# Attention work of three successive tiles emitted at one place of a fused attention and gated-MLP kernel

## The chip, the cores and the metric

The kernel runs on one core of a Trainium2 chip. The metric is the device time in microseconds (us) of one execution; before the change it is 1166.69 us, the median of 3 runs (1166.23 to 1167.01). Five engines run side by side, each with its own queue of instructions in order: TensorE (PE: matmuls; PEld is its weight load), VectorE (DVE), ScalarE (ACT), GpSimd (POOL) and SyncE (SP, which issues the DMA transfers). They wait for each other through semaphores.

## What is computed

Chunked attention with memory keys, a gated MLP with a sigmoid gate and a second MLP that multiplies by its own sigmoid, in float32:

```python
# attention: 4 batches, 8 heads, 768 tokens, head dimension 64
for c in range(24):                            # chunks of 32 queries
    k_full = concat(mem_k, k[c*32-16 : c*32+40])   # 8 + 56 keys at most
    v_full = concat(mem_v, v[c*32-16 : c*32+40])
    s = q_c @ k_full.T / 8
    a = exp(s - max(s)); a = a / (sum(a) + 1e-9)
    out_c = a @ v_full
# first MLP: 3072 tokens, 512 -> 1536 -> 512
y = (sigmoid(x @ w_gate) * (x @ w_val)) @ w_out
# second MLP: 3072 tokens, 512 -> 2048 -> 512
h = y @ w_in;  result = (h * sigmoid(h)) @ w_out2
```

## The kernel before

**Tiles and blocks.** The 3072 tokens are 24 attention tiles of 128 tokens (six to a sequence, so the tiles 0, 6, 12 and 18 begin one) and six token blocks of 512, block 0 to block 5 (`bi`), of four tiles each. The attention of block 0 runs at the start. After that the first MLP runs block by block, and the attention of the four tiles of block `bi + 1` is interleaved with the MLP of block `bi`. The second MLP follows at the end, with nothing of the attention in it. Weights arrive as 64-bit numbers and are joined, and float32 values are split into two parts (a cast on ScalarE, then a subtraction, `split`), so that three matmuls of part times part stand for one product.

**A round.** For a block, a loop of 12 rounds runs over the slices `f` of the 1536 hidden columns. A round emits, in this order: the gate projection (`pg`, 12 wide matmuls of 128x512, L263) and its sigmoid on ScalarE (L273); step 0; the value projection (`pv`, 12 wide matmuls, L263); step 1; the gate product on VectorE (`sg<-pv,sg`, L277) and its split; the output matmuls of the round before (`y`, 12 wide matmuls, L90, L92, L94); step 2. So a block has 36 steps. `pg` and `pv` share a PSUM ring of two buffers (`ps_m`): a gate projection can begin when the sigmoid of the round before has read its buffer, a value projection when the gate product of the round before has.

**Head of a block.** In round 0 the output matmuls complete the previous block. Directly behind them the four finished tiles are copied from PSUM to SBUF, two by ScalarE (L530) and two by VectorE (L532), and stored (L533). These copies take their buffers from the same ring of three (`sg`) as the sigmoids; VectorE's second copy and the next sigmoid wait until a store has freed a buffer.

**Steps.** A step first runs its attention events (`run_events`), then, in block 0, the preparation of the first MLP's weights, and from block 1 on, in steps 1 and 2 of a round, one piece of the preparation of the second MLP's weights (`prepare2`). These pieces follow each other in a cycle of seven: a join, a join, four sums, and four half splits. A join is a rescale on ScalarE (L107) and three VectorE instructions (L115, L118, L122); the sums are four VectorE instructions (L478); a half split is a cast on ScalarE, a subtraction on VectorE and a store on SP (L486, or L492 with two DMAs). The half splits use one buffer (`co`), so a cast waits until the store before it has landed.

**Attention events of a tile.** Four kinds, at steps that `events` fixes:
- scores: 16 small matmuls into a PSUM tile `sc` (L189; tiles at the edge of a sequence get a mask, L197, L199), on VectorE the maximum (L202) and a subtraction into `e` (L203), on ScalarE the exponential (L204, for which ScalarE loads another function table than for the sigmoid); then two loads on SP, queries and keys of the next tile;
- norm: row sum, add, reciprocal and multiplication on VectorE (L210 to L213);
- turn: four transposes of `e` on TensorE into a PSUM tile `pt` (L219), copied by ScalarE to `at` (L220);
- pv: 16 small matmuls of `at` with the values into a PSUM tile `px` (L229), transposed into the block's input by VectorE (L236); then two loads on SP, values of the next tile. In the text below this is called the product, to keep it apart from the value projection.

The tiles `sc`, `pt` and `px` come from one PSUM ring of two buffers (`ps_a`); `e`, `at`, and the loaded queries, keys and values have one buffer each.

**What sets the order.** The schedule is manual: each engine's queue holds its instructions in the order in which the program emits them. Before the change tile `jj` of a block has its scores at step 3 + 8 `jj`, norm at 5 + 8 `jj`, turn at 7 + 8 `jj` and product at 9 + 8 `jj`. No two events share a step.

Of the kernel before, what the change touches and what calls it, by code (L numbers as in the profile page):

```python
# [23 lines left out]
NF1, NF2 = FF1 // P, FF2 // P  # L24
# [23 lines left out]
def moe_kernel(ctx: ExitStack, tc: tile.TileContext, qh, kh, vh, wg, wv, wo, w2i, w2o, out):  # L48
# [132 lines left out]
    def att_scores(t, ps_sc, e):  # L181
        sc = ps_sc(f"sc{t}")
        scv = sc.rearrange("p (c2 a k) -> p c2 a k", c2=2, a=4)
        qb, kt = q_t.pop(t), k_t.pop(t)
        for c2 in range(2):
            for a in range(4):
                for cp in range(2):
                    c = 2 * c2 + cp
                    nc.tensor.matmul(  # L189
                        scv[cp * 64 : cp * 64 + 64, c2, a],  # L190
                        qb[:, 4 * a + c].rearrange("p u q -> p (u q)"),
                        kt[:, a, c],
                        start=True,
                        stop=True,
                    )
        if t % TPB == 0:
            nc.vector.memset(scv[0:64, 0, :, NMEM : NMEM + LEFT], NEG)  # L197
        if t % TPB == TPB - 1:
            nc.vector.memset(scv[64:128, 1, :, WIN - RIGHT : WIN], NEG)  # L199
        s3 = sc.rearrange("p (g k) -> p g k", k=WIN)  # L200
        m = att.tile([P, 8, 1], F32, tag="m", name=f"m{t}", bufs=2)
        nc.vector.tensor_reduce(m, s3, axis=AX.X, op=ALU.max)  # L202
        nc.vector.tensor_tensor(out=e, in0=s3, in1=m.to_broadcast([P, 8, WIN]), op=ALU.subtract)  # L203
        nc.scalar.activation(out=e, in_=e, func=AF.Exp, scale=SCALE)  # L204
        e_t[t] = e

    def att_norm(t, eng=nc.vector):
        e = e_t[t]
        r = att.tile([P, 8, 1], F32, tag="r", name=f"r{t}", bufs=2)
        nc.vector.tensor_reduce(r, e, axis=AX.X, op=ALU.add)  # L210
        nc.vector.tensor_scalar_add(r, r, 1e-9)
        nc.vector.reciprocal(r, r)
        eng.tensor_tensor(out=e, in0=e, in1=r.to_broadcast([P, 8, WIN]), op=ALU.mult)  # L213

    def att_turn(t, ps_pt, at):
        e = e_t.pop(t).rearrange("p g k -> p (g k)")
        pt = ps_pt(f"pt{t}")
        for i in range(4):
            nc.tensor.transpose(pt[:, i * P : (i + 1) * P], e[:, i * P : (i + 1) * P], ident)  # L219
        nc.scalar.copy(at.rearrange("p a b q -> p (a b q)"), pt)  # L220
        at_t[t] = at

    def att_pv(t, ps_px, xt, off):
        at, vb = at_t.pop(t), v_t.pop(t)
        px = ps_px(f"px{t}")
        for c in range(4):
            for j in range(4):
                q0 = 64 * (c % 2) + 32 * (j % 2)
                nc.tensor.matmul(  # L229
                    px[32 * j : 32 * j + 32, c * P : (c + 1) * P],  # L230
                    at[:, c // 2, j // 2, q0 : q0 + 32],
                    vb[c * len(vb) // 4][:, :, c % (4 // len(vb)), j],
                    start=True,
                    stop=True,
                )
        nc.vector.transpose(  # L236
            out=xt[:, :, off : off + P].rearrange("p k (c q) -> p c k q", c=4),
            in_=px.rearrange("p (c k q) -> p c k q", c=4, k=4),
        )
# [3 lines left out]
    def x32_tile(name):  # L243
        return hold[0].tile([P, KT, 512], F32, tag="x32", name=name)
# [38 lines left out]
    with tc.manual_schedule():  # L283
# [17 lines left out]
        def at_tile(t):  # L301
            return att.tile([P, 2, 2, P], F32, tag="at", name=f"at{t}", bufs=1)

        def e_tile(t):
            return att.tile([P, 8, WIN], F32, tag="e", name=f"e{t}", bufs=1)
# [7 lines left out]
        for t in range(1, n0):  # L313
            i = 5 + 2 * (t - 1)
# [62 lines left out]
        def prefetch(t):  # L377
            if t < NTILE:
                att_load_qk(t, qA, k_tile(t))

        def prefetch_v(t):
            if t < NTILE:
                att_load_v(t, vA)

        idle(22)
        for i in range(n0 + 2):
# [3 lines left out]
            if 0 <= i - 2 < n0:  # L390
                at = hold[0].tile([P, 512], F32, tag="sg", name=f"at{i - 2}", bufs=3)
# [26 lines left out]
        events = {}  # L418
        for bi in range(NB1 - 1):
            n = BLOCKS1[bi + 1] // P  # L420
            for jj in range(n):
                t = starts1[bi + 1] // P + jj
                at = 3 * NF1 * bi + 3 + 24 * jj // max(n - 1, 1)
                for d, what in ((0, "scores"), (2, "norm"), (4, "turn"), (6, "pv")):
                    events.setdefault(at + d, []).append((what, t, bi + 1, jj))

        def run_events(i):
            for what, t, bn, jj in events.get(i, []):
                if what == "scores":
                    att_scores(t, ps_a, e_tile(t))  # L430
                    prefetch(t + 1)
                elif what == "norm":
                    att_norm(t)
                elif what == "turn":
                    att_turn(t, ps_a, at_tile(t))
                else:
                    if bn not in x32:
                        x32[bn] = x32_tile(f"x32_{bn}")
                    att_pv(t, ps_a, x32[bn], jj * P)
                    prefetch_v(t + 1)  # L440
# [179 lines left out]
        turn = [0]  # L620
# [181 lines left out]
        for bi, n in enumerate(BLOCKS1):  # L802
# [6 lines left out]
            for f in range(NF1):  # L809
                it = 3 * (bi * NF1 + f)  # L810

                def steps(i):
                    run_events(it + i)
                    if bi == 0:
                        feed1.step()
                    elif (it + i) % 3 != 0:
                        next(prep, None)
                    if last and (i == 2 and 1 < f < NF1):

                        if f >= 3:  # L820
                            next(xgen, None)
# [117 lines left out]
```

## Time and profile before

| | us |
|---|---|
| median of 3 runs | 1166.69 |
| lowest, highest | 1166.23, 1167.01 |
| the profiled execution | 1165.85 |
| span of its instructions | 1164.1 |
| TensorE busy in the span | 1138.2 |
| VectorE, ScalarE, GpSimd busy | 695.6, 487.4, 124.5 |
| mean granted clock of TensorE, as a share of full speed | 0.996 |

The profile is of one execution on the chip. Times of instructions are in us from the start of the span. Matmuls are pipelined, and their ends are modelled: the cost of one in a row of many is the distance from start to start, not its duration. A bracket behind a row of the timeline is the time its engine sat idle before it, and what ended that.

### The profile page before, as it was taken

Reading aid. Unit: us, or ns where it says so; the run is one execution under the profiler, and the core shown is the slowest. Engines: PE = TensorE matmul, PEld = TensorE weight load, DVE = VectorE, ACT = ScalarE, POOL = GpSimd, SP = SyncE. Lnnn points to the kernel's source line nnn. Section 1 sums busy time; section 2 is a strip of 40 time slices with the busy share of each in tenths; the row PEclk is TensorE's granted clock in tenths of the full one; section 3 lists DMA queues with packets and bytes.
Section 4 is the critical chain, followed back from the end, with each engine's and each line's share of the span. In section 5 each row is a group of like instructions: output and inputs, shape, how many; then the busy total and the mean of one; then the engine's idle time right before and its main releaser. Section 6 shows DMA issues by size and latency. Waiting matters only on the chain.

```text
span 1164.1 us, 16020 instructions
## 1 busy us (share of the span) xinstructions
PE 1138.2 (98%) x6319; PEld 927.7 (80%) x6319; DVE 695.6 (60%) x965; ACT 487.4 (42%) x708; POOL 124.5 (11%) x94
## 2 busy tenths in 40 slices
PE   8889999999999999999999999999999999999998
PEld 7667777888888888888887888888888888888887
DVE  7999965455555554554564534347944369634665
ACT  3555544334434433443343224445434454344442
POOL 2545530000000000000000001111001110011000
PEclk9999999999999999999999999999999999999999
DMA  9777767667656666766565356566655575655552
GB/s 314 244 238 246 242 218 238 208 206 227 224 194 212 219 227 194 242 213 203 199 205 211 120 188 199 190 239 237 228 199 192 205 282 215 227 193 203 208 204 86
DMA packets 79210, 248.51 MB, mean 213 GB/s; under 512 B 7584, under 2 KB 23968, under 8 KB 69920
## 3 DMA queue, kind: packets, MB, share of 16 engines
q1 hardware_dynamic: 79136, 247.49, 62.4%
q8 instruction: 50, 0.82, 0.3%
q14 instruction: 24, 0.20, 0.0%
HBM read 199.23 MB, written 48.23 MB: 213 GB/s over the span
## 4 chain that ended last, share of the span: by engine, by line
PE 83%; DVE 12%; DMA 3%; issue 1%; ACT 0%; SPq 0%; DVEq 0%; ACTq 0%
PE o L771 20%; PE c L658 20%; PE pv L263 13%; PE pg L263 13%; PE y L90 5%; PE y L92 5%; PE y L94 5%; PE sc L189 1%; PE px L229 1%; DVE t_wg L122 1%; DVE t_wo L122 1%; DVE t_wv L122 1%; DVE stg_wv L118 1%; DVE stg_wo L118 1%; DVE stg_wg L118 1%; DMA v<-in_vh_dram 1%
## 5 line engine op out<-in xcount | busy, mean ns | idle before, releaser
L658 PE MATMUL c<-xp,wr 128*128 128x512 f32 x1008 | 229.1, 389 | 0.0
L771 PE MATMUL o<-gf,wr 128*128 128x512 f32 x1008 | 229.0, 389 | 0.0
L263 PE MATMUL pv<-x,w 128*128 128x512 f32 x864 | 216.1, 400 | 13.0 <-DVE sg L277 11.4
L658 PEld LDWEIGHTS c<-xp,wr 128*128 128x128 f32 x1008 | 189.2, 188 | 39.3
L771 PEld LDWEIGHTS o<-gf,wr 128*128 128x128 f32 x1008 | 189.2, 188 | 39.3
L263 PE MATMUL pg<-x,w 128*128 128x512 f32 x864 | 210.6, 392 | 1.6 <-POOL x L85 0.9
L263 PEld LDWEIGHTS pv<-x,w 128*128 128x128 f32 x864 | 162.9, 191 | 51.9 <-issue 14.3
L263 PEld LDWEIGHTS pg<-x,w 128*128 128x128 f32 x864 | 160.4, 188 | 38.2 <-ACT x L82 1.5
L85 DVE TENSOR_TENSOR gf<-g,gf 128x1024 fp32r<-128x1024 f32 x84 | 103.8, 1239 | 49.9 <-ACT gf L82 49.6
L82 ACT CAST gf<-g 128x1024 fp32r<-128x1024 f32 x84 | 88.1, 1053 | 86.9 <-PE o L771 73.3
L678 POOL TENSOR_TENSOR s<-s,s 128x512 f32<-128x512 f32 x24 | 35.9, 1497 | 820.7 <-ACT s L677 820.7
L82 ACT CAST g<-sg 128x512 fp32r<-128x512 f32 x72 | 44.7, 621 | 156.8 <-DVE sg L277 156.8
L273 ACT ACTIVATE sg<-pg 128x512 f32<-128x512 f32 x72 | 42.9, 596 | 74.8 <-PE pg L263 61.7
L630 DVE TENSOR_TENSOR s<-c,s 128x512 f32<-128x512 f32 x48 | 33.2, 691 | 65.1 <-PE c L658 63.1
L90 PE MATMUL y<-g,wor 128*128 128x512 f32 x240 | 66.3, 397 | 0.6 <-DVE y L532 0.6
L85 DVE TENSOR_TENSOR g<-sg,g 128x512 fp32r<-128x512 f32 x60 | 41.5, 692 | 41.7 <-ACT g L82 41.7
L92 PE MATMUL y<-g,wor 128*128 128x512 f32 x240 | 64.3, 390 | 0.0
L94 PE MATMUL y<-g,wor 128*128 128x512 f32 x240 | 64.2, 389 | 0.0
L277 DVE TENSOR_TENSOR sg<-pv,sg 128x512 f32<-128x512 f32 x72 | 49.3, 684 | 21.3 <-PE pv L263 21.2
L633 DVE TENSOR_TENSOR g<-g,g 128x1024 f32<-128x1024 f32 x48 | 58.4, 1216 | 0.0
L636 ACT ACTIVATE g<-s 128x512 f32<-128x512 f32 x48 | 30.3, 632 | 54.1 <-DVE s L630 54.1
L92 PEld LDWEIGHTS y<-g,wor 128*128 128x128 f32 x240 | 45.1, 188 | 9.6
(120 smaller groups left out, 1127.3 us busy)
## 6 DMA issues: line engine op xcount, KB each, us to landing
wr<-w2o_d SPq DMA_DIRECT2D x42, 1024.0 KB, 4.8
wor<-wo_d SPq DMA_DIRECT2D x60, 512.0 KB, 4.7
wr<-w2i_d SPq DMA_DIRECT2D x24, 1024.0 KB, 5.0
wr<-w2i_d SPq DMA_DIRECT2D x24, 768.0 KB, 4.4
w2o_d<-coo SPq DMA_DIRECT2D x56, 256.0 KB, 2.8
w2i_d<-coi SPq DMA_DIRECT2D x24, 512.0 KB, 3.0
qA<-in_qh_dram SPq DMA_DIRECT2D x21, 512.0 KB, 4.9
k<-in_kh_dram SPq DMA_DIRECT2D x21, 512.0 KB, 5.5
```

What stands on the lines that cost most here:

```text
L82: nc.scalar.copy(hi, src)
L85: lo_eng.tensor_tensor(out=lo, in0=src, in1=hi.bitcast(F32), op=ALU.subtract)
L90: nc.tensor.matmul(o, w_hi, x_hi, start=first, stop=False)
L92: nc.tensor.matmul(o, w_hi, x_lo, start=False, stop=False)
L94: nc.tensor.matmul(o, w_lo, x_hi, start=False, stop=last)
L263: nc.tensor.matmul(o[:, :n], w[:, pw, kt * P : (kt + 1) * P], x[kt][:, px, :n], start=i == 0, stop=i == len(steps) - 1,)
L273: nc.scalar.activation(out=sg[:, :n], in_=psg[:, :n], func=AF.Sigmoid)
L277: nc.vector.tensor_tensor(out=sg[:, :n], in0=psv[:, :n], in1=sg[:, :n], op=ALU.mult)
L633: nc.vector.tensor_tensor(out=o, in0=a, in1=b_, op=ALU.subtract)
L658: nc.tensor.matmul(o, w[:, pw, i % 4, kt * P : (kt + 1) * P], X[i][:, px, kt], start=first and j == 0, stop=j == 5, skip_group_check=not f ...
L678: nc.gpsimd.tensor_tensor(out=s5, in0=s5, in1=s1, op=ALU.add)
L771: nc.tensor.matmul(c[at[i], dp], w[:, pw, pl, dp * P : (dp + 1) * P], f[:, px, pl], start=i in (A11, S1, S2) and pp == 0 and j == 0, stop= ...
```

## The change

The steps of the events change for the tiles that are computed beside blocks 1 to 4 (`bi` not 0): scores at 2 + 6 `jj`, norm at 4 + 6 `jj`, turn at 8 + 6 `jj`, product at 14 + 6 `jj`. All matmuls of the attention then stand in step 2 of a round, behind the output matmuls. Where several events share a step they run in the order of the tiles: product of tile `t - 2`, turn of tile `t - 1`, scores of tile `t`. Beside block 0 the steps stay as they were, and no events share a step there.

```diff
                 t = starts1[bi + 1] // P + jj
                 at = 3 * NF1 * bi + 3 + 24 * jj // max(n - 1, 1)
-                for d, what in ((0, "scores"), (2, "norm"), (4, "turn"), (6, "pv")):
+                gaps = (("scores", 0), ("norm", 2), ("turn", 4), ("pv", 6))
+                if bi:
+
+                    at = 3 * NF1 * bi + 2 + 6 * jj
+                    gaps = (("scores", 0), ("norm", 2), ("turn", 6), ("pv", 12))
+                for what, d in gaps:
                     events.setdefault(at + d, []).append((what, t, bi + 1, jj))
 
         def run_events(i):
-            for what, t, bn, jj in events.get(i, []):
+            for what, t, bn, jj in sorted(events.get(i, []), key=lambda e: e[1]):
                 if what == "scores":
```

## Rows read from the trace of the kernel before

**Rows 1.** Busy time by stretch, block 2: us, engines' busy (instructions), clock, DMA share, GB/s.
```profile
271.50:381.47 109.97, 109.97 (x705) 89.33 (x704) 59.48 (x109) 43.95 (x67) 0.00 (x0) 1.00 0.65 214
```
**Rows 2.** The page's costliest groups, second MLP's wide matmuls: busy us, mean ns.
```profile
L771 PE MATMUL o<-gf,wr 128*128 128x512 f32 x1008 | 229.0, 389 | 0.0
```
**Rows 3.** Timeline of TensorE in block 1: start, us, instructions merged by line.
```profile
214.37 1.07 PE L94 MATMUL y<-g,wor 128*128 128x512 f32 x4
215.37 1.08 PE L229 MATMUL px<-vA,at 128*32 128x128 f32 x32
216.38 3.01 PE L263 MATMUL pg<-x,w 128*128 128x512 f32 x12
...
222.04 1.15 PE L189 MATMUL sc<-k,qA 128*64 128x64 f32 x32
223.12 1.19 PE L90 MATMUL y<-g,wor 128*128 128x512 f32 x4
224.16 1.08 PE L92 MATMUL y<-g,wor 128*128 128x512 f32 x4
```
**Rows 4.** Timeline of TensorE in block 0's attention, small matmuls alone.
```profile
19.38 0.60 PE L219 MATMUL pt<-ident,e_w 128*128 128x128 f32 x4
19.91 1.08 PE L229 MATMUL px<-v,at 128*32 128x128 f32 x32
```
**Rows 5.** Timeline of VectorE, a product behind the output matmuls in block 1.
```profile
216.52 0.72 DVE L236 STREAM_TRANSPOSE x<-px 128x512 f32<-128x512 f32 x1 [1.64 <-PE px L229]
```
**Rows 6.** Timeline of ScalarE, head of block 1.
```profile
172.91 0.67 ACT L107 ACTIVATE stg_w2i<-stg_w2i 128x512 f32<-128x512 f32 x1
...
179.25 0.63 ACT L204 ACTIVATE e<-e 128x512 f32<-128x512 f32 x1 [1.35 <-DVE e L203]
```
**Rows 7.** Timeline of VectorE, head of block 1.
```profile
175.33 0.69 DVE L532 COPY y<-y 128x512 f32<-128x512 f32 x1 [2.40 <-DMA yd<-y]
...
177.80 0.69 DVE L202 TENSOR_REDUCE m<-sc 128x8 f32<-128x512 f32 x1
...
179.13 1.54 DVE L478 TENSOR_TENSOR fi<-fi 128x256 f32<-128x256 f32 x4
...
182.57 0.68 DVE L210 TENSOR_REDUCE r<-e 128x8 f32<-128x512 f32 x1
...
183.73 0.69 DVE L213 TENSOR_TENSOR e<-e,r 128x512 f32<-128x512 f32 x1
```
**Rows 8.** Timeline of TensorE, second value projection and turn of block 1.
```profile
181.33 3.01 PE L263 MATMUL pv<-x,w 128*128 128x512 f32 x12
184.56 0.63 PE L219 MATMUL pt<-ident,e 128*128 128x128 f32 x4 [0.22 <-DVE e L213]
```
**Rows 9.** Timeline of VectorE, head of block 2.
```profile
282.42 0.69 DVE L532 COPY y<-y 128x512 f32<-128x512 f32 x1 [2.33 <-DMA yd<-y]
...
289.27 0.69 DVE L85 TENSOR_TENSOR coo<-fo,coo 128x512 fp32r<-128x512 f32 x1 [3.92 <-ACT coo L82]
289.88 0.68 DVE L277 TENSOR_TENSOR sg<-pv,sg 128x512 f32<-128x512 f32 x1
```
**Rows 10.** Timeline of SyncE's DMA issues, head of block 2.
```profile
283.74 0.91 SPq L492 DMA_DIRECT2D w2o_d<-coo  x2
```
**Rows 11.** The page's DMA issues, half splits' stores: KB each, median us to landing.
```profile
w2o_d<-coo SPq DMA_DIRECT2D x56, 256.0 KB, 2.8
```
**Rows 12.** Timeline of VectorE, heads of blocks 3 and 4.
```profile
393.94 0.69 DVE L532 COPY y<-y 128x512 f32<-128x512 f32 x1 [2.83 <-DMA yd<-y]
...
502.41 0.69 DVE L532 COPY y<-y 128x512 f32<-128x512 f32 x1 [2.18 <-DMA yd<-y]
```
**Rows 13.** Timeline of TensorE, second value projections of blocks 2, 3 and 4.
```profile
291.85 2.88 PE L263 MATMUL pv<-x,w 128*128 128x512 f32 x12
...
401.82 2.88 PE L263 MATMUL pv<-x,w 128*128 128x512 f32 x12
...
511.99 2.88 PE L263 MATMUL pv<-x,w 128*128 128x512 f32 x12
```

## The prediction

> **What bounds the kernel now.** I read three views. First the busy time by stretch: block 2 (271.50 to 381.47) lasts 109.97 us and TensorE is busy in all of it, at a granted clock of 1.00, the higher of the two levels [rows 1]. The other three blocks that the change touches look alike: hardly a wait is left there that the change could remove. A gain can come only from TensorE's own instructions, a loss from any new wait, and both reach the end of the run in full. Second, the order of TensorE's work, to price one insertion of attention work between two runs of wide matmuls [rows 2, 3, 4]. Third, the queues of VectorE and ScalarE at the head of a block, where the slack is smallest [rows 6 to 13]; the reader is to see there which instruction stands in line behind which.
>
> **The change part by part.** Instructions are neither added nor removed. In blocks 1 to 4, 16 tiles in all, the scores go from step 3+8j to 2+6j, the normalisation from 5+8j to 4+6j, the turn from 7+8j to 8+6j and the product from 9+8j to 14+6j. So a block has six places with matmuls in place of twelve: scores alone (step 2), turn+scores (8), product+turn+scores (14 and 20), product+turn (26), product alone (32). The loads behind the scores (queries, keys: two) and the product (values: two) move with them on SP's queue. They still have six steps, two rounds of 36 wide matmuls, before they are needed, so I cost them at nothing.
>
> Switches. A wide matmul takes 229.0/1008 = 0.227 us, four 0.91 [rows 2]. Block 2 has 432 of them, 98.1 us; the rest, 11.9, is four tiles, so 3.0 us for the three insertions of a tile [rows 1, 2]. In one place: going in costs 1.00 - 0.91 = 0.09, the product 1.01, the scores 1.08, coming back 1.04 - 0.91 = 0.13 [rows 3]. Four transposes ahead of another shape took 0.53 [rows 4]; after a product the first is slowed too, so I take 0.58 (0.45 to 0.65). Sum 2.89: a triple saves 0.1. For a pair I take 0.05 (0 to 0.1). Per block 2 x 0.1 + 2 x 0.05 = 0.3, over four blocks -1.2 us (-2 to 0). The Trainium skill (TensorEngine Tiling (Array Packing), Key Properties) says that a change of tiling mode drains TensorE. By that rule a place that holds three shapes still pays inside itself; the trace agrees with 0.09 going in and 0.13 coming back [rows 3], and by the rule the saving stays at the 1.2 above; without drains inside a place it would be that of rival (b).
>
> PSUM wait. The attention's PSUM ring has two buffers, and a triple takes three: product in one, turn in the other, scores again in the product's. So the scores wait until VectorE has transposed the product out. That transpose took 0.72 and began 0.07 after the product's modelled end, which is 1.08 after its start [rows 3, 5]; from a VectorE end to a waiting TensorE 0.14 (184.42 to 184.56) [rows 7, 8]. 1.08+0.07+0.72+0.14 = 2.01 after the product's start, against 1.01+0.58 = 1.59 without the wait: 0.41 a triple, eight triples, +3.3 us. Lower end 0.3 each (a shorter release), +2.5. The upper end is a VectorE still busy when the product ends. In the four places where a product already stands right after the output matmuls (the first is the row) it starts at once, and the same spacing of six steps after a tile's scores holds in every triple; but in some it had hardly been idle. I allow 0.6 more each, +8. Behind the waiting scores TensorE has the wide matmuls of the next projection, so all of it is on the path; the loads for the next tile on SP only wait with it.
>
> Head of the block. Here is the larger term. At the start of a block the finished outputs of the block before are copied from PSUM, two by ScalarE and two by VectorE, and VectorE's second waits for a store to free its buffer: 2.40 us at 175.33 [rows 7]. Before, the first tile's scores stood behind the first part of the next round, and its maximum, subtraction and exponential came after that round's sigmoid and after a preparation step. Now they stand directly behind those copies, ahead of the preparation step and of the sigmoid, and the normalisation comes one step earlier, which puts it ahead of the gate product of the second round (L277). That product frees the PSUM buffer of the next value projection.
>
> Block 1: VectorE's copy ends at 176.02. From the maximum's start to the exponential's end is 179.88-177.80 = 2.08 [rows 6, 7], so the exponential ends at 178.1. The preparation's rescale (0.67, at 172.91 before [rows 6]) is now queued behind it on ScalarE: 178.8. VectorE's two remaining join instructions, 0.7 each as the maximum, end at 180.2; the normalisation, 182.57 to 184.42 = 1.85, at 182.05; four sums, 1.54, at 183.5; the gate product, 0.68 as in block 2 [rows 9], at 184.2. The value projection then starts at 184.3 in place of 181.33 [rows 8]: +3.0 (2.7 to 3.2). TensorE first meets a part of this one projection earlier, since the sigmoid too is behind the exponential, and its table load.
>
> Block 3, the same chain: copy end 394.63, exponential 396.7, rescale 397.4, join 398.85, normalisation 400.7, a whole join (1.8, from 176.0 to 177.80 in block 1 [rows 7]) 402.5, gate product 403.15; the projection at 403.25 in place of 401.82 [rows 12, 13]: +1.4 (1.2 to 1.6).
>
> Blocks 2 and 4: the step behind the exponential is half of a split (ScalarE cast, VectorE subtract) and the next half must wait for its store to land. Block 2: copy end 283.11 [rows 9], exponential 285.3 with the mask of a sequence's first tile, cast and subtract (0.69 each, the subtract's row) 286.7. The store then leaves at 286.7, not at 283.74; the gate product began 6.14 after that store's issue [rows 9, 10]. Kept, it begins at 292.8 and the projection at 293.6 in place of 291.85 [rows 13]: +1.7. With a store that lands in 2.8, the median [rows 11], plus half a microsecond for the second issue and 1.3 for cast and subtract, it is 291.3, and +0.2. I take +0.9 (0 to 1.7), as the loads issued just ahead compete with the store. Block 4: copy end 503.10, store at 506.6, by the same two readings 0 and +1.4 against 511.99 [rows 12, 13]; I take +0.6. Heads together 3.0+0.9+1.4+0.6 = +5.9 (3.9 to 7.9). One small gain: the turn's 0.22 wait at 184.56 [rows 8] goes, since it now comes four steps after the normalisation.
>
> In the other rounds the normalisation after scores at a place of this kind is already seen in every block (scores at step 11), without a wait on TensorE [rows 1], so I cost these at nothing; a round whose split waits longer for a store could add some tenths.
>
> Sum: -1.2+3.3+5.9-0.2 = +7.8 us. On the profiled execution, 1165.85, that is 1173.65. That execution is 0.84 below the median of the three runs (1166.69), so for the median 1174.5. With the ends of the terms -2+2.5+3.9-0.2 = +4.2 and 0+8+7.9-0.2 = +15.7.
>
> **The rivals.** (a) The heads absorb the move: the copies' stores land some 3 us earlier, or the preparation step gets ahead of the exponential. Then -1.2+3.3-0.2 = +1.9, 1168.6, within what can be told from no change. Against it: the order on both engines is the order of emission, and the 2.40 us wait for the store is before the moved instructions. (b) Not slower, but faster: the matmuls of one place run together without paying for the change of shape inside it, which saves about 0.22 at each inner boundary, six a block, 24 in all, 5.3 us, and neither heads nor triples wait: 1166.7-5.5 = 1161.2. It decides only if the product is out of PSUM before the four transposes end, that is if 2.01 is in truth under 1.6. For it speaks only the halved number of places; against it the 0.53 [rows 4], and that the transpose alone takes 0.72. (c) VectorE is regularly late at the triples, because its gate chain still waits for a split's store: 1.2 more at each of eight, +9.6, 1184. For it: the long waits for stores, as VectorE's 3.92 at 289.27 [rows 9]; against it the four places named above. (d) The change does less than it says: only two of six places hold three tiles; that is in the sum.
>
> **How the numbers follow.** Forecast 79%, (a) 9%, (b) 3%, (c) 9%. Predicted 1174.5 us; the range from 1169.5 to 1180.5 leaves out (a), (b), most of (c) and the far ends of the triples' wait. What can be told from no change is 0.2%, 2.3 us (1164.4 to 1169.0). Slower by more: the forecast, (c) and little of (a), 0.88; the same 0.09; faster 0.03.
>
> **What would show it.** In the changed kernel's waits of TensorE: the scores (L189) for VectorE's transpose (L236), eight times, 0.3 to 0.5 each; the gate projection for ScalarE's sigmoid in block 1, as the larger part of its 3.0; the value projection for L277 in the second round of the heads. Block 1 should be about 3.5 us longer, the others 1 to 2. Wrong: no wait at the heads, or triples that wait over 1 us.

## The result, and the profile after

The changed kernel takes 1182.57 us (median of 4 runs, 1180.63 to 1184.80) against 1166.50 of the kernel before: ratio 1.0138 (95% interval 1.0126 to 1.0151), 16.1 us slower. The forecast was 1174.5 with a range that ended at 1180.5. The direction and most places of the loss were as forecast (the head of block 5 was not), and its size was twice that. The profiled execution took 1181.57 us, its span is 1179.8, which is 15.7 longer than before.

The work is the same. These two lines of the page are the span and the busy times:

```profile
span 1179.8 us, 16010 instructions
...
PE 1141.6 (97%) x6319; PEld 931.2 (79%) x6319; DVE 696.5 (59%) x965; ACT 487.6 (41%) x708; POOL 124.6 (11%) x94
```

TensorE is busy for 3.4 us more than before (1138.2), and idle for 12.3 more (38.2 against 25.9): so some of the loss is waiting, and some is the same matmuls running longer. Where, the stretches show, one for each of the blocks 1 to 4, from the first gate projection of one to that of the next, in the columns of [rows 1]:

```profile
159.94:274.57 114.63, 111.80 (x705) 90.67 (x704) 61.43 (x111) 43.53 (x66) 1.29 (x1) 0.99 0.70 232
274.57:387.29 112.72, 110.14 (x706) 89.57 (x704) 58.09 (x106) 43.32 (x66) 0.00 (x0) 1.00 0.61 201
387.29:500.99 113.70, 110.44 (x705) 89.44 (x704) 60.42 (x110) 43.91 (x68) 0.00 (x0) 1.00 0.66 220
500.99:615.42 114.43, 111.79 (x705) 90.74 (x704) 60.88 (x110) 43.63 (x67) 0.00 (x0) 0.99 0.57 185
```

Before, these blocks lasted 110.96, 109.97, 110.17 and 109.97. They are 3.7, 2.7, 3.5 and 4.5 longer, 14.4 of the 15.7 us; block 2, 109.97 in [rows 1], now has 2.58 in which TensorE stands still. In blocks 1 and 4 it is also busy 1.2 to 1.8 longer, at a lower mean clock. The waits of TensorE from block 1 to the head of block 5 (instruction and what it waited for: us in total, times, longest):

```profile
PE pv L263 <- DVE sg L277: 4.5, 3, 2.1
PE pg L263 <- ACT sg L273: 3.5, 2, 1.9
PE y L90 <- DVE y L537: 2.5, 1, 2.5
PE sc L189 <- ACT at L220: 2.0, 3, 0.7
PE sc L189 <- DVE x L236: 1.3, 5, 0.3
```

In the same stretch before there were two waits, 0.6 and 0.2 long. The first two lines are heads of blocks (8.0 us), the third is the head of block 5, and the last two are the eight triples (3.3). The timeline of TensorE in the head of block 1 and in two triples:

```profile
179.68 4.61 PE L263 MATMUL pg<-x,w 128*128 128x512 f32 x12 [1.90 <-ACT sg L273]
184.13 2.93 PE L263 MATMUL pv<-x,w 128*128 128x512 f32 x12
...
206.81 1.07 PE L94 MATMUL y<-g,wor 128*128 128x512 f32 x4
207.81 1.08 PE L229 MATMUL px<-vA,at 128*32 128x128 f32 x32
208.82 0.66 PE L219 MATMUL pt<-ident,e 128*128 128x128 f32 x4
209.73 1.15 PE L189 MATMUL sc<-k,qA 128*64 128x64 f32 x32 [0.25 <-DVE x L236]
210.81 3.02 PE L263 MATMUL pg<-x,w 128*128 128x512 f32 x12
...
229.70 1.15 PE L189 MATMUL sc<-k,qA 128*64 128x64 f32 x32 [0.67 <-ACT at L220]
```

The gate projection waits 1.90 for the sigmoid, and then its 12 matmuls take 4.45 from start to start of the next run, in place of 2.72 for an undisturbed run. The stretches from 180 to 182, 182 to 184 and 184 to 186 have the granted clock as the third number from the end:

```profile
180.00:182.00 2.00, 2.00 (x7) 1.56 (x6) 1.92 (x6) 0.00 (x0) 0.00 (x0) 0.58 0.90 346
182.00:184.00 2.00, 2.00 (x7) 1.58 (x6) 1.31 (x3) 0.96 (x2) 0.00 (x0) 0.56 0.78 317
184.00:186.00 2.00, 2.00 (x11) 1.60 (x10) 0.98 (x2) 0.78 (x2) 0.00 (x0) 1.00 0.08 33
```

Behind the wait the clock is at the lower level, 1.2 GHz, for most of the projection, and then back at 2.4. So this wait cost 1.90 and another 1.73. The other heads, in the timeline of TensorE (blocks 2, 3, 3, 4 and 5):

```profile
296.73 3.02 PE L263 MATMUL pv<-x,w 128*128 128x512 f32 x12 [1.65 <-DVE sg L277]
...
406.66 3.03 PE L263 MATMUL pg<-x,w 128*128 128x512 f32 x12 [1.59 <-ACT sg L273]
410.44 3.01 PE L263 MATMUL pv<-x,w 128*128 128x512 f32 x12 [0.75 <-DVE sg L277]
...
523.64 4.33 PE L263 MATMUL pv<-x,w 128*128 128x512 f32 x12 [2.14 <-DVE sg L277]
527.76 1.43 PE L90 MATMUL y<-g,wor 128*128 128x512 f32 x4
...
632.41 0.50 PE L90 MATMUL y<-g,wor 128*128 128x512 f32 x1 [2.55 <-DVE y L537]
```

Block 4 has a second fall of the clock: 4.12 start to start in place of 2.72, and 0.35 more in the `y` behind it. A stretch inside it:

```profile
525.50:527.50 2.00, 2.00 (x6) 1.54 (x6) 0.69 (x1) 1.11 (x2) 0.00 (x0) 0.50 0.78 259
```

The sum: waits 8.03 + 3.28 + 2.55 = 13.86; lower clock 1.73 + 1.40 + 0.35 = 3.48; less what block 1's head, its turn and block 5 already lost before (0.44, 0.22 and 0.65). The first of these three is read from the value projection of [rows 8] and [rows 13], which is the third of its block, not the second: it starts 20.79 after the block's start, and 20.35 in blocks 2 to 4 of before. That makes 16.0. From the start of block 1 to the end the changed kernel took 16.3 longer (1019.86 against 1003.56); the span has only 15.7 because block 1 began 0.6 earlier, at 159.94 in place of 160.54. So nothing is left that saved switches could account for, and 0.3 of the loss is not located.

### The profile page after: what moved, and what is told of

Same layout as the page of the kernel before. It is cut to its first block, busy times and chain, and to the rows that moved or that the text cites. A ratio compares the mean times of both kernels' runs of the same rounds, so it can differ in the third digit from the quotient of the medians.

```text
span 1179.8 us, 16010 instructions
## 1 busy us (share of the span) xinstructions
PE 1141.6 (97%) x6319; PEld 931.2 (79%) x6319; DVE 696.5 (59%) x965; ACT 487.6 (41%) x708; POOL 124.6 (11%) x94
## 4 chain that ended last, share of the span: by engine, by line
PE 77%; DVE 13%; DMA 6%; ACT 2%; issue 1%; DVEq 0%; SPq 0%; ACTq 0%
PE o L776 19%; PE c L663 19%; PE pg L263 12%; PE pv L263 12%; PE y L92 4%; PE y L90 4%; PE y L94 4%; DMA yd<-y 2%; DVE t_wg L122 1%; PE px L229 1%; DVE t_wo L122 1%; DMA w2i_d<-coi 1%; PE sc L189 1%; DVE t_wv L122 1%; DVE stg_wv L118 1%
## 5 line engine op out<-in xcount | busy, mean ns | idle before, releaser
L263 PE MATMUL pg<-x,w 128*128 128x512 f32 x864 | 214.3, 397 | 5.1 <-ACT sg L273 3.5
L277 DVE TENSOR_TENSOR sg<-pv,sg 128x512 f32<-128x512 f32 x72 | 49.3, 685 | 25.9 <-PE pv L263 25.6
L85 DVE TENSOR_TENSOR coi<-fi,coi 128x512 fp32r<-128x512 f32 (+1 forms) x32 | 19.9, 623 | 74.0 <-ACT coi L82 74.0
```

The costliest lines, as they stand in the source:

```text
L85: lo_eng.tensor_tensor(out=lo, in0=src, in1=hi.bitcast(F32), op=ALU.subtract)
L263: nc.tensor.matmul(o[:, :n], w[:, pw, kt * P : (kt + 1) * P], x[kt][:, px, :n], start=i == 0, stop=i == len(steps) - 1,)
L277: nc.vector.tensor_tensor(out=sg[:, :n], in0=psv[:, :n], in1=sg[:, :n], op=ALU.mult)
```

## The experiments

The theory after the comparison: the loss is the heads (VectorE and ScalarE in order behind an output copy that waits for its store), the triples' PSUM wait, a lower clock behind the longest waits, and a late head of block 5; the shared places themselves save nothing. The rivals: the loads, which I had cost at nothing, are the larger cause; or the loss comes from the earlier normalisation; or the places do save, and the waits cost more than they show. Edits are to the changed kernel, unless said otherwise. Each ratio is to the kernel before on the same chip, whose median there was 1166.2 to 1166.7; differences from the changed kernel are between chips.

**heads_back**: the first tile of a block gets its old places behind the preparation step.

```diff
+                    if jj == 0:
+                        gaps = (("scores", 1), ("norm", 3), ("turn", 6), ("pv", 12))
```

> The changed kernel, but in blocks 1 to 4 the first tile's scores and normalisation stand at steps 3 and 5 again; turns, products and all other tiles stay as changed. Theory H (the loss sits at the heads of the blocks, where the first tile's maximum, exponential and normalisation stand ahead of preparation, sigmoid and gate product; with the clock that falls after the two longest waits this is about 11 of the 16 us): 1169 to 1172 us, no wait of a projection over 0.3 us in the second round of a block, the eight waits of the scores still there with 3.3 us together. Rival S (the six places themselves cost, by what VectorE and ScalarE must do behind each): over 1178.

Measured 1170.53, ratio 1.0035 (1.0022 to 1.0048), inside the expectation. This one tile of four carries 12 of the 16 us. Of the heads one wait of 0.6 is left, no clock falls there, and block 5's wait is 1.6. The scores still wait eight times, 3.7 in all.

**product_apart**: the product one step earlier, so that no place holds three.

```diff
-                    gaps = (("scores", 0), ("norm", 2), ("turn", 6), ("pv", 12))
+                    gaps = (("scores", 0), ("norm", 2), ("turn", 6), ("pv", 11))
```

> The changed kernel, but the product stands one step earlier, at 13 + 6j, behind the value projection and ahead of the output matmuls: no place holds three tiles any more, so no PSUM buffer is wanted twice in one place. Theory H: only the eight waits of the scores go, 3.3 us, so 1178 to 1180.5. Rival S: most of the 16 us goes, 1167 to 1171.

Measured 1178.05, 1.0094 (1.0079 to 1.0109), as expected. The scores wait nowhere, in the waits of TensorE over the same blocks:

```profile
PE pv L263 <- DVE sg L277: 4.5, 3, 2.0
PE pg L263 <- ACT sg L273: 2.1, 1, 2.1
PE y L90 <- DVE y L537: 1.7, 1, 1.7
```

That is 4.5 less than the changed kernel. In the profile the triples' 3.3 of waits are gone, and with them the 1.59 of block 3's gate projection and 0.9 in block 5, while the clock falls behind three waits of the heads (1.79, 1.96 and 2.08) in place of two. The other heads stand without the triples.

**both_back**: both edits together.

> Both edits together: first tile's scores and normalisation at steps 3 and 5, product one step earlier; turn of one tile and scores of the next still share a place. Theory H with the reading that places save nothing on TensorE: 1166 to 1168.5. With the saving that was forecast (1.2 us and more): under 1165.5. Rival S: well over 1168.

Measured 1168.43, 1.0016 (1.0006 to 1.0025), at the upper end. There are nine places in a block here against twelve before, and the kernel isn't faster than before. Waits of 0.4 to 1.0 are left, and 1.5 in block 5: the two edits are not the whole of the loss.

**heads_only**: the kernel before, with only the first tile's scores and normalisation one step earlier in blocks 1 to 4.

```diff
+                first = bi and jj == 0
-                for d, what in ((0, "scores"), (2, "norm"), (4, "turn"), (6, "pv")):
+                for d, what in ((-first, "scores"), (2 - first, "norm"), (4, "turn"), (6, "pv")):
```

> The kernel before, with one part of the change alone: in blocks 1 to 4 the first tile's scores go from step 3 to 2 and its normalisation from 5 to 4. Theory H: nearly all of the loss but the triples' waits, 1175 to 1180, with the same waits of gate and value projections in the second round and the clock falling after some of them. Rival S: 1166 to 1168.

Measured 1172.16, 1.0055 (1.0035 to 1.0074), runs from 1170.71 to 1175.61: less than I expected by then, and close to the head term of the prediction (5.5 against 5.9). The waits:

```profile
PE pv L263 <- DVE sg L277: 3.1, 3, 1.9
PE pg L263 <- ACT sg L273: 2.0, 1, 2.0
PE y L90 <- DVE y L533: 0.7, 1, 0.7
```

By blocks they are 2.35, 1.88, none and 0.87, where the forecast had 3.0, 0.9, 1.4 and 0.6: that the totals are close is luck. Block 5's wait is as before, so in the changed kernel it has another cause. Block 3 has none, but its first split came 4.8 after the block's start here and 6.2 before, behind a block 2 that was 2.2 longer, so this run doesn't test the 1.4. The clock did not fall here in the profiled execution: the gate projection behind the wait of 1.99 ran at 1.00.

**loads_behind**: the loads that follow the scores and the product are emitted behind the preparation step (and its store) in place of ahead of it.

```diff
-                    prefetch(t + 1)
+                    later.append((prefetch, t + 1))
...
-                    prefetch_v(t + 1)
+                    later.append((prefetch_v, t + 1))
...
+                    while later:
+                        load, t = later.pop(0)
+                        load(t)
```

> The changed kernel, with one thing more: the loads that scores and product issue (queries, keys, values of the next tile) are emitted behind the preparation piece of the same step, so that on SP's queue they no longer stand ahead of that piece's store. Theory L (what the forecast left out at the heads is that these loads delay the half splits' stores, so the next cast waits longer, and behind it the gate product): the waits of the value projections in the second round of blocks 2 and 4 (1.65 and 2.14 us) shrink below 1 and the clock does not fall there, block 3's 2.3 falls to about 1.4; 1174 to 1178 us. Rival O (the order on ScalarE and VectorE alone): no more than 1 us less than the changed kernel, over 1181.

Measured 1177.29, 1.0096 (1.0081 to 1.0111): 5 us of the 16 are won back. Block 2's wait goes from 1.65 to 0.39 and block 4's from 2.14 to none, so the loads ahead of the store are what delayed these two heads. Block 1 gets a wait of 1.10 of its `y` in exchange, and keeps its 2.07 with the lower clock behind it: the loads are a part of it, not the whole. What the loads do to the store is seen on SyncE's queue in the head of block 2 (first the changed kernel, as in [rows 10], then loads_behind):

```profile
283.78 2.77 SPq L538 DMA_DIRECT2D yd<-y  x2
286.64 0.38 SPq L162 DMA_DIRECT2D qA<-in_qh_dram  x1
287.07 0.44 SPq L163 DMA_DIRECT2D k<-in_kh_dram  x1
289.76 0.89 SPq L497 DMA_DIRECT2D w2o_d<-coo  x2
```
```profile
291.62 0.88 SPq L499 DMA_DIRECT2D w2o_d<-coo  x2
```

Before, the store left at 283.74, ahead of both loads and 12.24 after the block's start. Now it leaves behind them, 15.19 after the start, as forecast (286.7, or 15.2). In loads_behind it leaves ahead of them and 15.18 after the start: so the loads don't hold up its issue. They hold up its landing, which took 4.4 us here and 5.6 in block 4, against 2.7 and 3.0 in loads_behind. The next cast of the split waits for it, on ScalarE and, behind that, on VectorE (first line ScalarE, block 2; second and third VectorE, block 2; last ScalarE, block 4), with the gate product at the end of the queue:

```profile
294.74 0.62 ACT L82 CAST coo<-fo 128x512 fp32r<-128x512 f32 x1 [3.81 <-DMA w2o_d<-coo]
```
```profile
295.39 0.69 DVE L85 TENSOR_TENSOR coo<-fo,coo 128x512 fp32r<-128x512 f32 x1 [3.88 <-ACT coo L82]
296.00 0.68 DVE L277 TENSOR_TENSOR sg<-pv,sg 128x512 f32<-128x512 f32 x1
```
```profile
521.64 0.62 ACT L82 CAST coi<-fi 128x512 fp32r<-128x512 f32 x1 [4.76 <-DMA w2i_d<-coi]
```

**norm_back**: the first tile's normalisation alone goes back, its scores stay.

```diff
+                    if jj == 0:
+                        gaps = (("scores", 0), ("norm", 3), ("turn", 6), ("pv", 12))
```

> The changed kernel, but the first tile's normalisation alone goes back from step 4 to 5, behind the gate product of the second round; its scores stay at step 2. Theory H: the sigmoid still waits for the exponential in block 1 (1.9 us and the clock), block 2 and 4 still wait for the store; only block 3's 0.75 at the value projection goes: 1180 to 1182.5. Rival N (the normalisation ahead of the gate product is what costs): 1172 to 1177.

Measured 1180.74, 1.0125 (1.0110 to 1.0140), as expected: about 2 us less than the changed kernel, though the runs of the two overlap (1178.88 to 1183.02 here). In block 3 only the second wait goes (0.75). The early scores make the head late, not the early normalisation.

**own_buffers**: two of the four output copies of a block, one of each engine, take a buffer of a ring that is idle there, so that VectorE's second copy need not wait for a store.

```diff
-                    y32 = tile_of(f"y32_{bi}_{dm}")
+                    own = dm < 2 and tile_of is sg_slot
+                    y32 = (t_slot if own else tile_of)(f"y32_{bi}_{dm}")
```

> The changed kernel, but two of the four copies of finished outputs take buffers of their own (two 512-wide buffers that stand idle after block 0), so neither VectorE's second copy nor the next sigmoid waits for a store. Theory H: the moved maximum, exponential and normalisation begin some 2.3 us earlier in every head: the sigmoid's wait in block 1 and the clock's fall behind it go, block 3's 2.3 go, blocks 2 and 4 lose most of theirs, and the wait of the output matmuls at the head of block 5 (2.5) goes: 1169 to 1174. Rival O: the sigmoid stands behind the exponential whatever the copies do: over 1178.

Measured 1168.89, 1.0022 (1.0013 to 1.0032), a little under the expectation. The order of emission is that of the changed kernel, and 13.7 of the 16.1 us are gone. (Some 2.2 of them the same buffers also give the kernel before, see before_own; against that, the new order still costs 4.9.) VectorE's timeline in the head of block 1:

```profile
172.12 1.28 DVE L538 COPY y<-y 128x512 f32<-128x512 f32 x2
173.32 0.68 DVE L202 TENSOR_REDUCE m<-sc 128x8 f32<-128x512 f32 x1
...
180.54 0.68 DVE L277 TENSOR_TENSOR sg<-pv,sg 128x512 f32<-128x512 f32 x1
```

The two copies stand back to back where [rows 7] has 2.40 of waiting; all that follows keeps its order and comes earlier. Left are three waits of 0.4 to 0.9 in the heads, 2.1 in all, and the scores' eight, 3.0.

**fill**: 16 transposes of the identity into a PSUM tile that nothing reads, behind the output matmuls of the second round of blocks 1 to 4. This adds some 7 us of TensorE work (1.91 each time).

```diff
+                if 0 < bi < NB1 - 1 and f == 1:
+                    fl = ps_a(f"fl{bi}")
+                    for _ in range(16):
+                        nc.tensor.transpose(fl[:, :P], ident, ident)
```

> The changed kernel with 16 transposes of the identity more on TensorE (1.75 us), into a PSUM tile of the attention's ring that nothing reads, behind the output matmuls of the second round of blocks 1 to 4, that is just ahead of the place where TensorE waits. Theory K (the granted clock falls because TensorE stands idle at these waits, and each fall costs 1.7 us behind it): the long waits shrink to some tenths, the clock does not fall behind them, 1178.5 to 1181. Rival: the fall has another cause, then the transposes come on top or change nothing: 1182 to 1186.

Measured 1176.36 (1176.24 to 1176.39), 1.0086 (1.0071 to 1.0101): better than expected, 6.2 us less than the changed kernel with 7 us more work. TensorE in the head of block 1:

```profile
178.36 1.91 PE L848 MATMUL fl<-ident 128*128 128x128 f32 x16
180.65 3.04 PE L263 MATMUL pg<-x,w 128*128 128x512 f32 x12 [0.39 <-ACT sg L273]
184.03 3.02 PE L263 MATMUL pv<-x,w 128*128 128x512 f32 x12 [0.34 <-DVE sg L277]
```

The sigmoid is as late as without the filler, but TensorE is not idle meanwhile, and the projection runs at its usual pace. The filler stands where the waits stood: +7.6 for it (4 x 1.91), -7.3 of waits in the heads (8.0 to 0.39 + 0.34), -3.5 as the clock doesn't fall, -1.5 in block 5 (2.55 to 1.05), -0.4 in the triples (3.3 to 2.9), together -5.1. From the start of block 1 to the end the two profiled executions are 5.9 apart (1013.99 against 1019.86), so 0.8 of the gain has no term here. Idle time that is filled costs nothing, and most of what is won is the clock's term. Why block 5 waits less I leave open.

**tail_back**: both_back, with the last tile's product of each block at its old step too.

```diff
+                    if jj == n - 1:
+                        gaps = (("scores", 0), ("norm", 2), ("turn", 6), ("pv", 13))
```

> First tile's scores and normalisation at steps 3 and 5 and all products one step earlier (13 + 6j), as in the run with both edits, but the last tile's product at step 33 again, as before the change. Theory T (at the end of a block the moved product puts its two value loads on SP ahead of a half split's store, the next cast waits longer, the gate product of the last round and with it the head of the next block come later): the wait of 0.43 us in the second round of block 3 goes, the wait of the output matmuls at the head of block 5 falls from 1.5 to about 0.7; 1166.7 to 1167.6. Rival: the later head of block 3 comes from elsewhere; then no change from 1168.4.

Measured 1165.79, 0.9995 (0.9986 to 1.0004), lower than expected, 2.6 less than both_back. So the product's place at the end of a block matters to the next head. In block 3 the cast of the half split in the first round, on ScalarE, first both_back, then tail_back:

```profile
389.76 0.41 ACT L82 CAST coi<-fi 128x256 fp32r<-128x256 f32 x1 [3.63 <-DMA w2i_d<-coi]
```
```profile
386.14 0.41 ACT L82 CAST coi<-fi 128x256 fp32r<-128x256 f32 x1 [1.10 <-DMA w2i_d<-coi]
```

The block began at 382.62 in the first and at 381.52 in the second, so the cast comes 7.1 and 4.6 after it; in the changed kernel it was 8.1 (395.36 against 387.29). The gate product and both copies stand behind this cast. Block 3 lasts 112.02 in both_back and 109.99 in tail_back: this explains block 3 and most of what both_back lacked; block 5 keeps a wait of 1.2. How the lateness arises in the changed kernel the end of its block 2 shows: the last product's transpose stands on VectorE at 379.13, ahead of a half split's subtraction at 379.77, and that split's store leaves 6.8 before the block's end, where it was 9.5 before the change. The product's loads add to it: in loads_behind the store leaves at the same 6.8, and the next cast comes 1.1 sooner.

**both_own**: both_back with own_buffers. **before_own**: the kernel before with own_buffers. **both_own_loads**: both_own with loads_behind.

> Both edits (first tile's scores and normalisation at 3 and 5, products at 13 + 6j) and two of the four copies of finished outputs in buffers of their own. Theory H: no wait at a head or at block 5; 1166.0 to 1167.2. If sharing a place saved TensorE what was forecast, under 1165.3.

> The kernel before, with two of the four copies of finished outputs in buffers of their own. Its only wait behind block 0 is 0.65 us of the output matmuls at the head of block 5, for one of these copies: 1165.5 to 1166.0, so 0.4 to 0.7 us less than before; the heads had slack, so no more than that. If heads bound the kernel before as well: 1 us or more less.

> As the run with both edits and own buffers, and the loads behind the preparation piece of their step. Theory L: the last waits behind a half split's store (0.4 to 1.0 us in blocks 1 to 3) shrink: 1165.5 to 1166.8. Rival: the loads behind the stores make block 1 wait, as they did alone (1.1 us of the output matmuls): 1167 to 1168.5.

Measured 1164.01, 1164.04 and 1163.82; 0.9981 (0.9972 to 0.9990), 0.9982 (0.9974 to 0.9991) and 0.9981 (0.9973 to 0.9990), all lower than expected. All three beat the kernel before by about 0.2%. In blocks 1 to 5 both_own and both_own_loads have no wait of TensorE at all, and before_own this one:

```profile
PE pt L219 <- DVE e L213: 0.2, 1, 0.2
```

With the waits gone on both sides, nine places in a block or twelve come out at the same time: block 2, without a wait in either, lasts 110.00 in both_own and 109.97 in before_own. These nine hold pairs, no triples. Two triples each stand in blocks 2 and 4 of heads_back, which last 110.39 and 110.37 with two waits of 0.25: some 109.9 without them, so a block with triples saves about 0.1. By the letter of two expectations the rivals came true (both_own is under 1165.3, and before_own over 1 us faster), but the second accounts for the first: the shared buffers cost the kernel before 2.2 us as well. Only 0.65 + 0.22 of that was listed as waiting. Block 1 is 0.9 shorter (its third value projection starts 20.42 after the block's start in place of 20.79), and so is what follows from block 5 on (its third gate projection starts at 16.33 in place of 17.26); so a head can lose some tenths that the view of the waits doesn't list. Where the rest of the 2.2 was lost is not shown. both_own_loads had no wait left that its loads could cause.

## Why the prediction was right in kind and wrong in size

**Bound and places: right, but for block 5.** TensorE has the same 6319 matmuls, every new wait reached the end in full, and the largest term was the heads. To the sum of +7.8 the trace adds 3.5 for the clock, 1.9 for the head of block 5, 1.7 for the other heads (8.03, less 0.44 lost before, against 5.9) and 1.2 for switches that were not saved: 16.1.

**Switches (-1.2): failed.** The sum above leaves nothing for it, pairs saved nothing between both_own and before_own, and a block with triples saved 0.1 in heads_back, where 0.3 was forecast. A triple shows why: 0.09 going in, 1.01 for the product, 0.66 for the turn, 1.08 for the scores and 0.14 coming back (from the rows of the first triple above) make 2.98 without the wait, against the 3.0 of three separate places. The turn behind a product takes 0.66 to its modelled end where [rows 4] has 0.60 (0.53 from start to start). And the turn has the wide matmuls' own shape, 128*128: a triple goes into the product's shape, out of it, into the scores' and out of it, as often as three places do, and a pair with a turn saves no change either. The Trainium skill's rule that a change of tiling mode drains TensorE (TensorEngine Tiling (Array Packing), Key Properties) agrees: there are as many changes apart as together, and they cost about the same. Counted so, the rule leaves nothing to save, and not the 1.2 that the prediction took from it.

**Triples (+3.3): right**, 3.3 measured, and in part by luck: none of the eight waits lies in the forecast 0.3 to 0.5. Five are of 0.25 for VectorE's transpose, the mechanism forecast. Three are of 0.67 for ScalarE: there the scores start 0.05 behind the end of its copy of the turn (229.70 and 229.65), so it seems that they got the PSUM buffer of the turn and not of the product; the profile doesn't number the buffers. Rival (c) fell; VectorE started the transpose of the product as soon as it ended, as here, first triple of block 1, against [rows 5]:

```profile
208.96 0.72 DVE L236 STREAM_TRANSPOSE x<-px 128x512 f32<-128x512 f32 x1 [0.24 <-PE px L229]
```

**Heads (+5.9): the chain was right, its price too low in blocks 2 to 4.** The order was as forecast, instruction for instruction: copy, maximum, subtraction, exponential, rescale, table load, sigmoid, and the normalisation ahead of the gate product. VectorE in block 1, answering to [rows 7], ended its gate product at 183.0; in the time of before, whose block 1 began 0.6 later, that is 183.6, and 184.2 was forecast (184.3 by its terms):

```profile
174.49 0.69 DVE L537 COPY y<-y 128x512 f32<-128x512 f32 x1 [2.34 <-DMA yd<-y]
175.10 0.68 DVE L202 TENSOR_REDUCE m<-sc 128x8 f32<-128x512 f32 x1
...
182.32 0.68 DVE L277 TENSOR_TENSOR sg<-pv,sg 128x512 f32<-128x512 f32 x1
```

Block 1's wait was 1.90, less than the 3.0 forecast, and the lower clock behind it cost another 1.73. Applied alone to the kernel before, this edit costs 5.5 (heads_only), though not in the blocks where it was forecast. What failed is what I left out of it:

- "They still have six steps [...] before they are needed, so I cost them at nothing": the loads have time, but the store behind them lands later (4.4 and 5.6 us in place of 2.7 and 3.0). At the heads of blocks 2 and 4 the prediction does name the loads as competing with the store, and I took 0.9 and 0.6, about the middle of two readings; the waits were 1.65 and 2.14. The old distance from store to next cast, which I had as the upper reading, held in block 2 (4.98 against 4.88 before) and was passed in block 4 (5.92). loads_behind, where these two waits become 0.39 and none, shows it.
- The tail: the product of a block's last tile moved from step 33 to 32, and I priced moved work only by its own matmuls. Block 3's first split came 1.9 later (8.1 against 6.2 after the block's start) and VectorE's copy behind it ended 1.7 later (14.86 against 13.16): there the head waited 2.34 where 1.4 was forecast. tail_back, one edit from both_back, takes the lateness away. In block 5 VectorE's copy waited 6.60 for a store in place of 5.58, 2.55 for TensorE; own_buffers shows that it hangs on the shared ring, since there it is gone. How much of it is the tail's I did not settle: tail_back still has 1.2, before 0.65.
- The clock behind the waits, +3.5, is no term of the sum at all. The trace of before had it to be read, in the timeline of TensorE in block 0, which I had used for other things only:

```profile
33.52 4.61 PE L263 MATMUL pv<-x,w 128*128 128x512 f32 x12 [1.43 <-ACT w L82]
...
52.69 3.01 PE L263 MATMUL pv<-x,w 128*128 128x512 f32 x12 [2.19 <-DVE sg L277]
...
121.70 4.47 PE L263 MATMUL pv<-x,w 128*128 128x512 f32 x12 [1.96 <-DVE sg L277]
```

A wait of 1.43 and one of 1.96 have a slow projection behind them, one of 2.19 has none: so a possible 1.7 for each long wait, not a certain one.

**Rivals and range.** (a) and (b) fell with the first waits at the heads, (c) with the row above, and (d) is not borne out: the emission is as the change says. The range stopped at +13.8 though its terms' own upper end was +15.7, and what was missing from the sum (loads, tail, clock) could only lengthen it; the time came out at +16.1.

## What to carry to other kernels

A move in the order of emission costs nothing only while every queue that it passes has slack at its tightest place, the DMA queue included: what stands behind the moved instructions is to be priced, not only the instructions. Where a short chain hangs behind a wait for a shared buffer, take that wait away first: here it made the old order 0.2% faster, and the new order's loss against it fell from 16.1 us to 4.9. Putting matmuls of different shapes side by side saved at most 0.1 us in a block of 110; here the changes of shape were to be counted, not the places.

## What the runs showed of the hardware that I had not expected

Behind some waits of about 2 us the clock fell to 1.2 GHz for the next 12 matmuls (4.45 in place of 2.72), behind others of the same length it did not. Of the waits over 1.5 us in the heads of blocks 1 to 4, in all these profiles, a slow projection follows those of 1.79, 1.90, 1.96, 2.01, 2.07, 2.08 and 2.14, and one at the usual pace those of 1.59, 1.65, 1.86, 1.88, 1.99 and 2.08. As in block 0 of before, the length of the wait alone doesn't tell. The kernels with such waits scatter by 3 to 5 us from run to run, and the longer runs tend to the lower mean clock (0.996, 0.993, 0.993 and 0.991 for the changed kernel's 1180.63, 1181.57, 1183.56 and 1184.80); the one with filler in place of idle time scatters by 0.15. Work that does nothing made the kernel 6.2 us faster. The Trainium skill (TensorE: Matmul & The Clock Gate, The HAM clock gate) says that the clock's default is the lower level and that activity releases it; the trace agrees as far as it goes, 0.58 behind 1.90 of idle time, and 1.00 before and after, but 1.00 also behind 1.99 in heads_only.
